# Routing steps of three batches on GpSimd, and pauses between VectorE's steps

## The chip, the cores and the metric

The kernel runs on one core of a Trainium2 chip. The core has TensorE (matmuls), VectorE, ScalarE and GpSimd, each with an instruction queue of its own that is worked off in order, and SyncE, which starts most DMAs. The metric is the device time of one execution in microseconds (us). Executions agree within about 0.2%, so a difference of about 2 us is what can be told from none.

## What is computed

Attention over 4 batches, 8 heads, 576 rows and 64 columns a head, in which a score counts only if it lies within `tau` of its row's maximum; then a mixture of 8 experts, for which each row's expert depends on the row before it; then a normalised feed-forward network with a residual.

```python
thresh = max(scores) - tau                      # per row
attn = softmax(where(scores >= thresh, scores, -1e9)) @ v

logits = x @ w_gate;  local = sigmoid(x @ w_local)
for s in range(S):                              # "sticky" routing, per batch
    e = argmax(logits[s]) if s == 0 or local[s] < 0.5 else prev_e
    prev_e = e
    p = softmax(logits[s])
    out[s] = p[e] * (relu(x[s] @ w1[e]) @ w2[e])

y = x + relu(layernorm(x) * g @ w_ch1) @ w_ch2
```

The routing of a batch turns 576 logit rows into each row's expert, its weight, and its place in a table sorted by expert. It runs on tiles of 128 partitions with 4 to 40 elements each (5 rows a partition, 8 experts), and some of up to 640.

## The kernel before

**Attention.** Work goes in pairs of heads, 16 in all, four to a batch. A pair has 9 *items* of 128 score rows, at positions 0 to 8. One pass of the main loop (`it`) works on several items at once. In a pass VectorE takes the row maximum of one item's scores (`mx`, L403, tile `mc` from `sm`) and masks another item's exponentials (`mask`, L452, `em`); ScalarE takes exponentials (`ex`, L446, `e`) and the upper half of a two-number split (L458, `hl`); GpSimd subtracts to get the lower half (L459, `hl`). TensorE computes the scores for the next maximum (`s_mm`, L399). There is one score tile `sm`, so these matmuls wait until `mx` has read the one before. Then it multiplies with V (`pv`, L474 to L478) for items two and more passes back, and computes transposed scores for the exponential (`t_mm`, L436, L441) into two buffers.

**Around it.** The same passes hold, in an order written out by hand, the preparation of the next pairs' Q, K and V (GpSimd: L306 `nat`, L363 `vl`), and the conversion of the feed-forward weights (`ffn_steps`: three VectorE steps L142, L144, L146 on `cv`, then ScalarE, then GpSimd's L158 `fw`). Conversions stand in the pairs 0 to 5, 7 to 9, 11 and 12. Pairs 6, 10, 13, 14 and 15 start none.

**Routing.** When the last pair of a batch has been stored and gated, `route(b)` runs as a generator: each pass of the loop takes it on to its next `yield`, at the end of the pass. Its matmuls ride in a corner of a score tile, and it goes on two passes later, when that tile's mask has run (`ride`, `alight`). For the first batch it starts in pair 5 at position 6, for the second in pair 9, for the third in pair 13, each time at position 6. The fourth batch's runs after attention, when GpSimd has nothing to do. The steps are named by their output tiles: `mxl`, `fr`, `eq`, `ex8` (with ScalarE's exponential), `eq` again, `idx`, `key`, `hold`, `loc`, the sum `smx`; then `holdr`, `erow`; then `e1`, `oh`; then `rk`, `pe`, `val4`, `pos`, `posi`, `lo`, `hi`; then `ol`, `oc`, `ov`.

Each engine does what its queue holds in the order in which the code was written, so a step that waits holds up everything behind it on its engine.

Of the kernel before, what the change touches and what calls it, by code (L numbers as in the profile page):

```python
# [13 lines left out]
ALU = mybir.AluOpType  # L14
AX = mybir.AxisListType
# [5 lines left out]
def kernel(  # L21
# [15 lines left out]
    nc = tc.nc  # L37
    B, H, S, D = q.shape
# [34 lines left out]
    val4 = const.tile([128, B, 5, 4], F16, name="val4")  # L73
# [156 lines left out]
    if True:  # L230
# [10 lines left out]
        oh = keep.tile([128, 6, 8], F16, name="oh")  # L241
# [318 lines left out]
        def route(b):  # L560


            inner = b < B - 1
# [13 lines left out]
            T = lambda nm, sh, dt=F32: rt_p.tile(sh, dt, name=nm)  # L577
            V = nc.vector
            L = lg[:, :, 0:8]
            mxl = T("mxl", [128, 5])  # L580
            V.tensor_reduce(out=mxl, in_=L, op=ALU.max, axis=AX.X)
            fr = T("fr", [128, 5])
            V.scalar_tensor_tensor(out=fr, in0=lg[:, :, 8], scalar=-1.5 * 2.0 ** -23, in1=first, op0=ALU.is_lt, op1=ALU.max)
            mb = mxl.unsqueeze(2).to_broadcast([128, 5, 8])
            eq = T("eq", [128, 5, 8])
            V.tensor_tensor(out=eq, in0=L, in1=mb, op=ALU.is_equal)
            ex8 = T("ex8", [128, 5, 8])
            V.tensor_tensor(out=ex8, in0=L, in1=mb, op=ALU.subtract)
            nc.scalar.activation(out=ex8, in_=ex8, func=AF.Exp)
# [3 lines left out]
            idx = T("idx", [128, 5])  # L593
            V.tensor_reduce(out=idx, in_=eq, op=ALU.min, axis=AX.X)
            key = T("key", [128, 5], F16)
            V.scalar_tensor_tensor(out=key, in0=idx, scalar=65.0, in1=fr, op0=ALU.add, op1=ALU.mult)
            hold = T("hold", [128, 4])
            V.tensor_scalar(out=hold, in0=key[:, 0:4], scalar1=0.0, scalar2=None, op0=ALU.is_equal)
            loc = T("loc", [128, 4], F16)
            V.tensor_tensor_scan(out=loc, data0=hold, data1=key[:, 0:4], initial=0.0, op0=ALU.mult, op1=ALU.add)  # L600
            sm = T("smx", [128, 5])
# [5 lines left out]

            V.tensor_scalar(out=sm, in0=sm, scalar1=1e-9, scalar2=2.0 ** -15, op0=ALU.add, op1=ALU.mult)
            row = (yield from product(f_row))[0:1, 0:192]
# [10 lines left out]

            V.tensor_tensor(out=ex8, in0=ex8, in1=sm.unsqueeze(2).to_broadcast([128, 5, 8]), op=ALU.mult)
            kb = yield from product(f_kb)
# [10 lines left out]

            V.tensor_tensor(out=ex8, in0=ex8, in1=oh[:, 0:5], op=ALU.mult)
            pe = T("pe", [128, 5])
# [3 lines left out]
            rk = T("rk", [128, 5, 8])  # L639
# [4 lines left out]
            V.tensor_reduce(out=pe, in_=ex8, op=ALU.add, axis=AX.X)  # L644
            V.tensor_tensor(out=rk, in0=rk, in1=oh[:, 0:5], op=ALU.mult)
            V.tensor_copy(out=val4[:, b, :, 1], in_=pe)
            pos = T("pos", [128, 5])
            V.tensor_reduce(out=pos, in_=rk, op=ALU.add, axis=AX.X)
            V.tensor_tensor(out=val4[:, b, :, 3], in0=pe, in1=val4[:, b, :, 1], op=ALU.subtract)
            posi = T("posi", [128, 5], I32)  # L650
            if inner:
                yield
            V.tensor_copy(out=posi, in_=pos)
            if not inner:
# [11 lines left out]
            if inner: yield  # L666
            oc = T("oc", [128, 5, 2 * E], F16)
            V.tensor_tensor(out=oc, in0=colid.unsqueeze(1).to_broadcast([128, 5, 2 * E]), in1=hi.unsqueeze(2).to_broadcast([128, 5, 2 * E]), op=ALU.is_equal)
            ov = T("ov", [128, 5, 4, 2 * E], F16)
            V.tensor_tensor(  # L670
                out=ov, in0=oc.unsqueeze(2).to_broadcast([128, 5, 4, 2 * E]), in1=val4[:, b].unsqueeze(3).to_broadcast([128, 5, 4, 2 * E]), op=ALU.mult)
# [121 lines left out]
    V = nc.vector  # L793
# [588 lines left out]
```

## Time and profile before

| | us |
|---|---|
| runs before, median of 3 (lowest, highest) | 1065.66 (1064.18, 1066.43) |
| the profiled execution | 1066.93 |
| its span, first to last instruction | 1065.0 |
| TensorE busy, matmuls | 999.8 (94%) |
| VectorE busy | 653.1 (61%) |
| ScalarE busy | 506.1 (48%) |
| GpSimd busy | 390.2 (37%) |
| mean granted TensorE clock | 0.971 of full speed |

The profile comes from one execution. In it PE is TensorE, PEld its weight loads, DVE VectorE, ACT ScalarE and POOL GpSimd; L459 is line 459 of the kernel. A busy share over the whole span mixes stages with different limits: attention takes about the first 390 us, and there GpSimd is far busier than its 37%. A bracket behind a row of the timeline gives the idle time of the engine before that instruction, and what ended it. A small instruction's duration contains the time for which it waited for a resource after it was started.

### The profile page before, as it was taken

To read this page: it belongs to the slowest core of one execution; us is meant where nothing else is said; L and a number is where in the kernel's file an instruction comes from. 1 tells how busy PE (TensorE), PEld (TensorE's weight loads), DVE (VectorE), ACT (ScalarE), POOL (GpSimd) and SP (SyncE) were. 2 spreads that over 40 slices of the span, in tenths; PEclk is the share of its full clock that TensorE was granted. 3 is DMA by queue.
4 is the path that set the end of the run, shared out by engine and by line. 5 is a ranking of instruction groups with operands and counts; after the bars stand their busy time and mean duration, and the time that the engine had idled before them with its cause. 6 is when DMAs were issued, how large, how long until landed. Compare 5 with 4: busy or idle time off the path is not lost. (4 is left out here: it accounts for less than half of the span.)

```text
span 1065.0 us, 23705 instructions
## 1 busy us (share of the span) xinstructions
PE 999.8 (94%) x9920; PEld 735.2 (69%) x9920; DVE 653.1 (61%) x1127; ACT 506.1 (48%) x791; POOL 390.2 (37%) x411
## 2 busy tenths in 40 slices
PE   6899998998999978999999979999999999999995
PEld 3678877786888866676667658585768567577572
DVE  7798888988888666697787757274333132231320
ACT  4688886786778655356566545153211011021110
POOL 3689897797788660233222210101000000000000
PEclk8999999999999996899999989999999999999998
DMA  7555634564342735768888765363110210111100
GB/s 177 143 141 148 137 95 125 121 172 129 92 86 57 192 130 171 230 201 276 268 287 306 237 205 167 119 224 117 37 30 31 60 30 31 40 41 41 30 12 22
DMA packets 124533, 137.34 MB, mean 129 GB/s; under 512 B 67450, under 2 KB 88954, under 8 KB 124416
## 3 DMA queue, kind: packets, MB, share of 16 engines
q1 hardware_dynamic: 98336, 116.43, 38.0%
q0 software_dynamic: 4960, 14.17, 3.6%
q10 hardware_dynamic: 21120, 5.13, 2.2%
q8 instruction: 79, 1.29, 0.5%
q14 instruction: 38, 0.31, 0.1%
HBM read 100.17 MB, written 19.94 MB: 113 GB/s over the span
## 5 line engine op out<-in xcount | busy, mean ns | idle before, releaser
L1121 PE MATMUL a<-nT,fw 128*128 128x256 f16 x1728 | 192.5, 274 | 6.3 <-DMA nT<-f 6.3
L1121 PEld LDWEIGHTS <-fw 128*128 128x128 f16 x1728 | 170.1, 98 | 29.3 <-issue 6.8
L459 POOL TENSOR_TENSOR hl<-em,hl 128x576 f16<-128x576 f32 x128 | 169.8, 1327 | 53.6 <-ACT hl L458 52.3
L1134 PE MATMUL y<-fw,hid 128*128 128x512 f16 x864 | 187.9, 379 | 0.0
L1134 PEld LDWEIGHTS <-hid 128*128 128x128 f16 x864 | 84.6, 98 | 100.4
L125 DVE SCALAR_TENSOR_TENSOR w<-stg,w 128x1024 f16<-128x1024 f32 x112 | 134.2, 1221 | 19.6 <-ACT w L124 19.3
L1124 ACT ACTIVATE hid<-a 128x512 f16<-128x512 f32 x72 | 42.7, 593 | 215.9 <-PE a L1121 214.0
L446 ACT ACTIVATE e<-s,t 128x576 f32<-128x576 f32 x144 | 106.2, 737 | 70.7 <-PE s L441 57.5
L1139 POOL DMA_INDIRECT out_dram<-xf x18 | 18.9, 1051 | 311.9 <-DVE xf L1138 311.9
L1012 PE MATMUL a<-xT,w 128*128 128x128 f16 (+1 forms) x1536 | 123.9, 243 | 2.0 <-DVE w L125 0.9
L1012 PEld LDWEIGHTS <-w 128*128 128x128 f16 x1536 | 114.2, 100 | 12.4 <-issue 1.6
L1033 PE MATMUL y<-w,hid 128*128 128x512 f16 x528 | 120.3, 386 | 1.5 <-DVE hid L1017 1.2
L403 DVE TENSOR_REDUCE mc<-sm 128x1 f32<-128x576 f32 x138 | 103.6, 751 | 24.4 <-PE sm L399 22.4
L124 ACT ACTIVATE w<-stg 128x1024 f16<-128x1024 f32 x112 | 114.3, 1051 | 8.8 <-DMA stg<-in_moe_w_dram 5.2
L452 DVE SCALAR_TENSOR_TENSOR em<-s,e 128x576 f32<-128x576 f32 x144 | 107.1, 745 | 9.0 <-POOL hl L459 7.4
L1125 DVE SCALAR_TENSOR_TENSOR hid<-a,hid 128x512 f16<-128x512 f32 x72 | 49.6, 689 | 102.6 <-ACT hid L1124 102.6
L1138 DVE SCALAR_TENSOR_TENSOR xf<-y,xf 128x512 f32<-128x512 f32 x18 | 12.5, 692 | 146.7 <-PE y L1134 146.7
L399 PE MATMUL sm<-qkt 128*128 128x288 f16 (+1 forms) x308 | 75.4, 291 | 24.4 <-DVE mc L403 21.3
L458 ACT ACTIVATE hl<-em 128x576 f16<-128x576 f32 x128 | 87.0, 680 | 18.6 <-DVE em L452 18.0
L1033 PEld LDWEIGHTS <-hid 128*128 128x128 f16 x528 | 51.8, 99 | 62.7 <-issue 3.6
L436 PE MATMUL s<-qkt 128*128 128x288 f16 (+1 forms) x320 | 90.6, 291 | 4.2 <-DVE em L452 3.2
L441 PE MATMUL s<-th,ind 128*128 128x128 bf16 (+5 forms) x960 | 92.6, 207 | 0.0
(288 smaller groups left out, 1805.3 us busy)
## 6 DMA issues: line engine op xcount, KB each, us to landing
stg<-in_moe_w_dram SPq DMA_DIRECT2D x112, 512.0 KB
stg<-in_moe_w_ch_dram SPq DMA_DIRECT2D x32, 512.0 KB
ys_d<-stg SPq DMA_DIRECT2D x6, 769.5 KB
xf<-ys_d SPq DMA_DIRECT2D x9, 513.0 KB
x_d<-xc SPq DMA_DIRECT2D x16, 256.0 KB
ku<-qkt SPq DMA_DIRECT2D x28, 144.0 KB
rawq<-in_q_dram SPq DMA_DIRECT2D x7, 512.0 KB
rawk<-in_k_dram SPq DMA_DIRECT2D x7, 512.0 KB
```

The source lines that it names most:

```text
L124: nc.scalar.activation(out=dst[:, 0, n], in_=t, func=AF.Copy, scale=scale)
L125: nc.vector.scalar_tensor_tensor(out=dst[:, 1, n], in0=t, scalar=scale, in1=dst[:, 0, n], op0=ALU.mult, op1=ALU.subtract)
L403: nc.vector.tensor_reduce(out=mcs[p % 2][:, j:j + 1], in_=mms.pop((p, j))[:, W0:W0 + 576], op=ALU.max, axis=AX.X)
L436: mm(o[:, W0 + 288 * c:W0 + 288 * c + 288], (kt, ku)[k][:, n], y, start=(k == 0), stop=False)
L441: mm(o[:, W0 + i:W0 + i + w], ind[:, t % 4, 0:o.shape[0]], y, start=False, stop=(i == of[-1][0]))
L446: nc.scalar.activation(out=e, in_=mst[p, j][:, W0:W0 + 576], func=AF.Exp, bias=t0, scale=SC)
L452: nc.vector.scalar_tensor_tensor(out=em, in0=ps[:, W0:W0 + 576], scalar=0.0, in1=e, op0=ALU.is_ge, op1=ALU.mult)
L459: nc.gpsimd.tensor_tensor(out=hl[:, 1], in0=em, in1=hl[:, 0], op=ALU.subtract)
L1012: nc.tensor.matmul(ps[:, f, :], t1[:, a, c, fc], x[:, h, i:i + N // 128, c, :], start=(n == 0), stop=(n == 11))
L1033: nc.tensor.matmul(ps, hid[:, x, f, 128 * i:128 * i + 128], t2[:, a, f, :], start=(n == 0), stop=(n == 23))
L1121: nc.tensor.matmul(ps[:, f, :], fw1[:, a, c, fc], x[:, h, :, c, :], start=(n == 0), stop=(n == 11))
L1134: nc.tensor.matmul(ps, hid[:, x, f, ts_], fw2[:, a, f, :], start=(n == 0), stop=(n == 47))
```

## The change

For the first three batches (`inner`) eight steps are issued on GpSimd (`G`) instead of VectorE: the subtraction for `ex8`, `hold`, the scaling of `smx`, the products of `ex8` with `smx` and with `oh`, the product of `rk` with `oh`, the remainder in `val4`, and `ov`. The sum `pos` moves behind the next `yield`. For the first two batches (`b < B - 2`) four more pauses (`gap`) spread VectorE's steps over more passes. The fourth batch's steps stay as they were.

```diff
--- before.py
+++ after.py
@@ -576,26 +576,34 @@
             lg, e1 = lgs[b % 2], e1s[b % 2]
             T = lambda nm, sh, dt=F32: rt_p.tile(sh, dt, name=nm)
             V = nc.vector
+            G = nc.gpsimd if inner else V
+
+            def gap():
+                if b < B - 2:
+                    yield
             L = lg[:, :, 0:8]
             mxl = T("mxl", [128, 5])
             V.tensor_reduce(out=mxl, in_=L, op=ALU.max, axis=AX.X)
             fr = T("fr", [128, 5])
             V.scalar_tensor_tensor(out=fr, in0=lg[:, :, 8], scalar=-1.5 * 2.0 ** -23, in1=first, op0=ALU.is_lt, op1=ALU.max)
             mb = mxl.unsqueeze(2).to_broadcast([128, 5, 8])
+            yield from gap()
             eq = T("eq", [128, 5, 8])
             V.tensor_tensor(out=eq, in0=L, in1=mb, op=ALU.is_equal)
             ex8 = T("ex8", [128, 5, 8])
-            V.tensor_tensor(out=ex8, in0=L, in1=mb, op=ALU.subtract)
+            G.tensor_tensor(out=ex8, in0=L, in1=mb, op=ALU.subtract)
             nc.scalar.activation(out=ex8, in_=ex8, func=AF.Exp)
             yield
             i8 = iota8.unsqueeze(1).to_broadcast([128, 5, 8])
             V.scalar_tensor_tensor(out=eq, in0=eq, scalar=-64.0, in1=i8, op0=ALU.mult, op1=ALU.add)
             idx = T("idx", [128, 5])
             V.tensor_reduce(out=idx, in_=eq, op=ALU.min, axis=AX.X)
+            yield from gap()
             key = T("key", [128, 5], F16)
             V.scalar_tensor_tensor(out=key, in0=idx, scalar=65.0, in1=fr, op0=ALU.add, op1=ALU.mult)
             hold = T("hold", [128, 4])
-            V.tensor_scalar(out=hold, in0=key[:, 0:4], scalar1=0.0, scalar2=None, op0=ALU.is_equal)
+            G.tensor_scalar(out=hold, in0=key[:, 0:4], scalar1=0.0, scalar2=None, op0=ALU.is_equal)
+            yield from gap()
             loc = T("loc", [128, 4], F16)
             V.tensor_tensor_scan(out=loc, data0=hold, data1=key[:, 0:4], initial=0.0, op0=ALU.mult, op1=ALU.add)
             sm = T("smx", [128, 5])
@@ -605,7 +613,7 @@
                 nc.tensor.matmul(t[0:1, 0:128], loc[:, 3:4], ident16)
                 nc.tensor.matmul(t[0:1, 128:192], key[0:64, 4:5], ident16[0:64, 0:64])
 
-            V.tensor_scalar(out=sm, in0=sm, scalar1=1e-9, scalar2=2.0 ** -15, op0=ALU.add, op1=ALU.mult)
+            G.tensor_scalar(out=sm, in0=sm, scalar1=1e-9, scalar2=2.0 ** -15, op0=ALU.add, op1=ALU.mult)
             row = (yield from product(f_row))[0:1, 0:192]
             yield from rest()
             holdr = T("holdr", [1, 192])
@@ -618,7 +626,7 @@
                 nc.tensor.matmul(t[:, 0:1], erow[:, 0:128], one1)
                 nc.tensor.matmul(t[0:64, 4:5], erow[:, 129:193], one1)
 
-            V.tensor_tensor(out=ex8, in0=ex8, in1=sm.unsqueeze(2).to_broadcast([128, 5, 8]), op=ALU.mult)
+            G.tensor_tensor(out=ex8, in0=ex8, in1=sm.unsqueeze(2).to_broadcast([128, 5, 8]), op=ALU.mult)
             kb = yield from product(f_kb)
             yield from rest()
             V.tensor_copy(out=e1[0:64, 4:5], in_=kb[0:64, 4:5])
@@ -631,7 +639,7 @@
                 for i in range(5):
                     nc.tensor.matmul(t[:, 8 * i + 8:48], ones16, oh[:, i:i + 1, :].to_broadcast([128, 5 - i, 8]), start=False, stop=(i == 4))
 
-            V.tensor_tensor(out=ex8, in0=ex8, in1=oh[:, 0:5], op=ALU.mult)
+            G.tensor_tensor(out=ex8, in0=ex8, in1=oh[:, 0:5], op=ALU.mult)
             pe = T("pe", [128, 5])
             R = (yield from product(f_R))[:, 0:48]
             yield from rest()
@@ -642,14 +650,16 @@
                 V.tensor_tensor(out=base_off, in0=R3[:, 5], in1=base_off, op=ALU.add)
                 yield
             V.tensor_reduce(out=pe, in_=ex8, op=ALU.add, axis=AX.X)
-            V.tensor_tensor(out=rk, in0=rk, in1=oh[:, 0:5], op=ALU.mult)
+            G.tensor_tensor(out=rk, in0=rk, in1=oh[:, 0:5], op=ALU.mult)
             V.tensor_copy(out=val4[:, b, :, 1], in_=pe)
             pos = T("pos", [128, 5])
-            V.tensor_reduce(out=pos, in_=rk, op=ALU.add, axis=AX.X)
-            V.tensor_tensor(out=val4[:, b, :, 3], in0=pe, in1=val4[:, b, :, 1], op=ALU.subtract)
+            if not inner:
+                V.tensor_reduce(out=pos, in_=rk, op=ALU.add, axis=AX.X)
+            G.tensor_tensor(out=val4[:, b, :, 3], in0=pe, in1=val4[:, b, :, 1], op=ALU.subtract)
             posi = T("posi", [128, 5], I32)
             if inner:
                 yield
+                V.tensor_reduce(out=pos, in_=rk, op=ALU.add, axis=AX.X)
             V.tensor_copy(out=posi, in_=pos)
             if not inner:
                 V.tensor_tensor(out=base_off, in0=R3[:, 5], in1=base_off, op=ALU.add)
@@ -666,8 +676,9 @@
             if inner: yield
             oc = T("oc", [128, 5, 2 * E], F16)
             V.tensor_tensor(out=oc, in0=colid.unsqueeze(1).to_broadcast([128, 5, 2 * E]), in1=hi.unsqueeze(2).to_broadcast([128, 5, 2 * E]), op=ALU.is_equal)
+            yield from gap()
             ov = T("ov", [128, 5, 4, 2 * E], F16)
-            V.tensor_tensor(
+            G.tensor_tensor(
                 out=ov, in0=oc.unsqueeze(2).to_broadcast([128, 5, 4, 2 * E]), in1=val4[:, b].unsqueeze(3).to_broadcast([128, 5, 4, 2 * E]), op=ALU.mult)
             yield
             def f_A(t):
```

The line numbers in the rows below are those of each kernel; behind the first edits those of the changed one are 5 to 11 higher.

VectorE, first batch, from the pass in which the routing has started. Before:

```order
L588 TENSOR_TENSOR ex8_2978<-lg0_158,mxl_2972 128x40
L403 TENSOR_REDUCE mc_168<-sm_2952 128x1
L452 SCALAR_TENSOR_TENSOR em_2984<-s_2921,e_2945 128x576
L592 SCALAR_TENSOR_TENSOR eq_2976<-eq_2976,iota8_76 128x40
L594 TENSOR_REDUCE idx_3053<-eq_2976 128x5
L596 SCALAR_TENSOR_TENSOR key_3055<-idx_3053,fr_2974 128x5
L598 TENSOR_SCALAR hold_3057<-key_3055 128x4
L600 SCALAR_TENSOR_TENSOR loc_3059<-hold_3057,key_3055 128x4
L602 TENSOR_REDUCE smx_3061<-ex8_2978 128x5
L403 TENSOR_REDUCE mc_168<-sm_2989 128x1
```

And now, from the mask two passes later on:

```order
L452 SCALAR_TENSOR_TENSOR em_3055<-s_2957,e_2977 128x576
L144 SCALAR_TENSOR_TENSOR cv_2701<-stg_2700,cv_2701 128x512
L146 SCALAR_TENSOR_TENSOR cv_2701<-stg_2700,cv_2701 128x512
L598 SCALAR_TENSOR_TENSOR eq_3047<-eq_3047,iota8_76 128x40
L600 TENSOR_REDUCE idx_3129<-eq_3047 128x5
L403 TENSOR_REDUCE mc_168<-sm_3060 128x1
L452 SCALAR_TENSOR_TENSOR em_3134<-s_3032,e_3053 128x576
L603 SCALAR_TENSOR_TENSOR key_3173<-idx_3129,fr_2974 128x5
```

Before, six routing steps stand between one mask and the next maximum (`mc`). Now `eq`'s second step and `idx` stand there, one pass later, where the two conversions of the weights (`cv`) stand too, and `key` stands alone in the pass after.

VectorE, two passes further, with `hold` now computed by GpSimd:

```order
L603 SCALAR_TENSOR_TENSOR key_3173<-idx_3129,fr_2974 128x5
L403 TENSOR_REDUCE mc_168<-sm_3139 128x1
L489 TENSOR_SCALAR rd_3179<-o_2989 128x5
L491 RECIPROCAL rd_3179<-rd_3179 128x5
L452 SCALAR_TENSOR_TENSOR em_3184<-s_3095,e_3132 128x576
L493 TENSOR_TENSOR xc_3178<-o_2989,rd_3179 128x5x64
L608 SCALAR_TENSOR_TENSOR loc_3213<-hold_3175,key_3173 128x4
L610 TENSOR_REDUCE smx_3215<-ex8_3049 128x5
```

`loc` has moved behind the normalisation of the first head's output (`rd`, `xc`).

GpSimd, third batch, around the split of V (`vl`). Before:

```order
L459 TENSOR_TENSOR hl_6746<-em_6744,hl_6746 128x576
L459 TENSOR_TENSOR hl_6780<-em_6778,hl_6780 128x576
L363 TENSOR_TENSOR vl0_157<-vraw_155,vh0_156 128x640
L459 TENSOR_TENSOR hl_6866<-em_6864,hl_6866 128x576
L459 TENSOR_TENSOR hl_6936<-em_6934,hl_6936 128x576
```

And now:

```order
L459 TENSOR_TENSOR hl_6746<-em_6744,hl_6746 128x576
L594 TENSOR_TENSOR ex8_6772<-lg0_158,mxl_6766 128x40
L459 TENSOR_TENSOR hl_6780<-em_6778,hl_6780 128x576
L363 TENSOR_TENSOR vl0_157<-vraw_155,vh0_156 128x640
L605 TENSOR_SCALAR hold_6855<-key_6853 128x4
L459 TENSOR_TENSOR hl_6866<-em_6864,hl_6866 128x576
L616 TENSOR_SCALAR smx_6859<-smx_6859 128x5
```

The third batch has no pauses: VectorE's `loc`, which reads `hold`, stands directly behind `key` there, as before. On GpSimd `hold` stands behind the split of V.

VectorE, first batch's late steps, in the pair with weight conversions that follows pair 6. Before, at its position 2:

```order
L452 SCALAR_TENSOR_TENSOR em_3710<-s_3649,e_3672 128x576
L142 TENSOR_SCALAR cv_3431<-stg_3430 128x512
L668 TENSOR_TENSOR oc_3766<-colid_78,hi_a_111 128x80
L670 TENSOR_TENSOR ov_3768<-oc_3766,val4_79 128x320
L403 TENSOR_REDUCE mc_161<-sm_3715 128x1
L452 SCALAR_TENSOR_TENSOR em_3773<-s_3686,e_3708 128x576
L144 SCALAR_TENSOR_TENSOR cv_3431<-stg_3430,cv_3431 128x512
```

And now, at the same position and the next:

```order
L142 TENSOR_SCALAR cv_3425<-stg_3424 128x512
L652 TENSOR_REDUCE pe_3604<-ex8_3049 128x5
L654 CAST val4_79<-pe_3604 128x5
L403 TENSOR_REDUCE mc_161<-sm_3703 128x1
L452 SCALAR_TENSOR_TENSOR em_3763<-s_3673,e_3693 128x576
L144 SCALAR_TENSOR_TENSOR cv_3425<-stg_3424,cv_3425 128x512
L662 TENSOR_REDUCE pos_3757<-rk_3697 128x5
L663 CAST posi_3759<-pos_3757 128x5
L671 TENSOR_SCALAR lo_a_110<-posi_3759 128x5
L672 TENSOR_SCALAR hi_a_111<-posi_3759 128x5
```

`oc` and `ov` were the routing's last steps there before. Now `pe`, the cast into `val4`, `pos`, `posi`, `lo` and `hi` stand beside the conversions, and the last steps follow later; `pos` reads the `rk` that GpSimd multiplies.

## Rows read from the trace of the kernel before

**Rows 1.** Profile page: engines, busy us, share of span, instructions.
```profile
PE 999.8 (94%) x9920; PEld 735.2 (69%) x9920; DVE 653.1 (61%) x1127; ACT 506.1 (48%) x791; POOL 390.2 (37%) x411
```

**Rows 2.** By stretch: length, busy us PE PEld DVE ACT POOL, clock, DMA, GB/s.
```profile
150.00:205.00 55.00, 49.15 (x696) 40.91 (x696) 48.55 (x98) 38.33 (x65) 39.95 (x41) 1.00 0.43 107
205.00:245.00 40.00, 39.15 (x589) 32.87 (x587) 35.25 (x55) 33.72 (x58) 36.93 (x36) 1.00 0.57 143
245.00:300.00 55.00, 49.54 (x690) 41.30 (x689) 47.76 (x97) 37.29 (x64) 39.12 (x39) 0.97 0.42 106
340.00:388.00 48.00, 43.96 (x648) 37.22 (x647) 36.09 (x85) 31.31 (x52) 32.08 (x35) 0.96 0.52 141
```

**Rows 3.** The same table, two short stretches with TensorE holes.
```profile
256.00:258.00 2.00, 1.35 (x12) 0.98 (x12) 1.97 (x4) 0.71 (x2) 0.00 (x0) 0.52 1.01 175
380.00:382.00 2.00, 0.78 (x16) 0.60 (x12) 2.00 (x3) 0.73 (x2) 0.40 (x1) 1.00 0.00 0
```

**Rows 4.** Timeline, first batch: start us, us, engine, line, operation, tiles.
```profile
157.92 0.94 DVE L596 SCALAR_TENSOR_TENSOR key<-idx,fr 128x5 f16<-128x5 f32 x1
...
158.90 1.21 DVE L598 TENSOR_SCALAR hold<-key 128x4 f32<-128x4 f16 x1
...
160.03 1.36 POOL L363 TENSOR_TENSOR vl<-vraw,vh 128x640 f16<-128x640 f32 x1
160.14 1.27 DVE L600 TENSOR_TENSOR_SCAN loc<-hold,key 128x4 f16<-128x4 f32 x1
```

**Rows 5.** Timeline, VectorE, fourth batch's routing.
```profile
416.94 0.17 DVE L598 TENSOR_SCALAR hold<-key 128x4 f32<-128x4 f16 x1
```

**Rows 6.** Groups by line: operation, tiles, count | busy us, mean ns | idle before.
```profile
L446 ACT ACTIVATE e<-s,t 128x576 f32<-128x576 f32 x144 | 106.2, 737 | 70.7 <-PE s L441 57.5 <-PE s L677 5.6 <-PE s L606 3.5
...
L458 ACT ACTIVATE hl<-em 128x576 f16<-128x576 f32 x128 | 87.0, 680 | 18.6 <-DVE em L452 18.0
...
L158 POOL TENSOR_TENSOR fw<-cv,fw 128x512 f16<-128x512 f32 x22 | 25.6, 1162 | 0.0
...
L414 POOL TENSOR_TENSOR r<-r,pt 128x12 f32<-128x12 f32 x15 | 3.3, 223 | 1.3
...
L867 POOL TENSOR_TENSOR ova<-oca,val 128x1280 f16<-128x1280 f16 x1 | 2.8, 2844 | 10.2 <-DVE oca L865 10.2
```

**Rows 7.** Timeline, third batch: GpSimd, TensorE, VectorE.
```profile
345.62 2.52 POOL L459 TENSOR_TENSOR hl<-em,hl 128x576 f16<-128x576 f32 x2
...
349.38 0.28 PE L399 MATMUL sm<-qkt 128*128 128x288 f16 x1 [1.45 <-DVE mc L403]
...
379.27 1.47 DVE L670 TENSOR_TENSOR ov<-oc,val 128x320 f16<-128x320 f16 x1
```

**Rows 8.** Timeline, VectorE, the pair before routing starts.
```profile
136.21 1.09 DVE L144 SCALAR_TENSOR_TENSOR cv<-stg,cv 128x512 int32<-128x512 int32 x1
137.33 1.65 DVE L146 SCALAR_TENSOR_TENSOR cv<-stg,cv 128x512 int32<-128x512 int32 x1
138.91 0.74 DVE L403 TENSOR_REDUCE mc<-sm 128x1 f32<-128x576 f32 x1
...
147.58 0.74 DVE L403 TENSOR_REDUCE mc<-sm 128x1 f32<-128x576 f32 x1
```

**Rows 9.** Timeline, GpSimd and TensorE, the same pair.
```profile
136.70 1.74 POOL L459 TENSOR_TENSOR hl<-em,hl 128x576 f16<-128x576 f32 x1
138.40 1.80 POOL L363 TENSOR_TENSOR vl<-vraw,vh 128x640 f16<-128x640 f32 x1
...
147.06 1.73 POOL L306 TENSOR_TENSOR nat<-rawq,nat 128x576 f16<-128x576 f32 x1
...
139.71 0.28 PE L399 MATMUL sm<-qkt 128*128 128x288 f16 x1
...
143.90 0.28 PE L399 MATMUL sm<-qkt 128*128 128x288 f16 x1
...
148.91 0.32 PE L399 MATMUL sm<-qkt 128*64 128x288 f16 x2
```

## The prediction, made before the result was known

> **What bounds the kernel now.** I read the engine totals first: TensorE is busy 94% of the span [rows 1], so time is won or lost where TensorE stands still. The table by stretch shows where [rows 2]. From 205 to 245 us, attention without routing, TensorE idles 0.85 us in 40. The stretches that hold the routing of the first three batches idle 5.85 us in 55, 5.46 in 55 and 4.04 in 48. At the rate of 205 to 245 us these would idle 1.2, 1.2 and 1.0, so routing costs 4.7, 4.3 and 3.0 us, 12.0 together. In the second batch the granted clock also fell behind the hole, to 0.52 [rows 3]: TensorE was busy 1.35 us there, of which 0.65 us is lost at half speed; I count 0.7. Nothing that this change does can win more than those 12.7 us.
>
> Then the timelines, for the reason. In the first batch VectorE's `key`, `hold` and `loc`, five elements a row, take 0.94, 1.21 and 1.27 us [rows 4]; in the fourth batch, where GpSimd is idle, `hold` takes 0.17 [rows 5]. `loc` ends at 161.41, when GpSimd's split of V (160.03 + 1.36) has just ended [rows 4]. So a small VectorE step that reads two SBUF tiles, casts, or scales from SBUF to SBUF waits until the GpSimd instruction in progress is over, and then GpSimd's next one runs before VectorE's next one. Five such steps in one item hold back the next `mx`, and TensorE's next scores wait for it.
>
> The Trainium skill, page "SBUF — State Buffer", section "Who interferes with whom", states the same: VectorE and GpSimd share a port pair, whoever starts first has it for the whole instruction, and the other blocks. The trace agrees (1.21 against 0.17 us). The rule speaks against the change as much as for it, since each step given to GpSimd is one more holder; and since it makes every meeting a race, a win by it would rest on who starts first: that is rival 1, 1061 us by the rows below, against the forecast, in which GpSimd does.
>
> **The change, part by part.** Eight steps a batch leave VectorE. On GpSimd seven cost some 0.27 us each (estimate: 0.22 for 12 elements, 1.26 for 576 [rows 6, 7], and these have at most 40) and `ov` 0.7 (2.84 for 1280 columns [rows 6], a quarter of that); 2.6 us a batch, no term by itself. What matters is where they stand in GpSimd's queue, and what waits for them. With the pauses the first two batches take four items more.
>
> I work it out on the pair from 127 to 149 us, which has the same attention work and weight conversions as the pair in which routing starts, and count what routing adds. Positions are those of items in a pair.
>
> *Position 7.* `mxl` and `fr`, two steps of 0.17 (as `hold` [rows 5]), stand ahead of `mx`: TensorE waits 0.35 us.
>
> *Position 8.* `eq` at the end of position 7 meets a GpSimd split and waits for its end: 0 to 1.26 us [rows 7], I take 0.75, a little over half. Then come two conversions and, new here, `eq`'s second step and `idx`. Before, the conversions took 1.09 and 1.65 us with their waits and `mx` began 2.70 us after the first of them [rows 8]; the first ran from 136.70 on, when GpSimd changed instruction [rows 9], so 0.6 of it is work. Now: rest of a split 1.2, conversion 0.6, split of V 1.36 [rows 4], conversion 0.6, the moved `ex8` 0.27, two steps of 0.2: 4.4 us. `mx` is late by 1.7 + 0.75 = 2.5 us, and the scores that began at 139.71 [rows 9] begin at 142.2. Of these 2.5 us 0.35 are counted: 2.15 us.
>
> *Position 2.* `loc` on VectorE now needs `hold` from GpSimd, and ScalarE's `exp` needs `ex8` from GpSimd. `ex8` stands behind the split of V, so `exp` can't start before 141.0 (the new `mx`, 141.4, less the two steps ahead of it); behind it in ScalarE's order wait `e` 0.74 and `hl` 0.68 [rows 6], and for that `hl` GpSimd's next split: 142.6. GpSimd then does that split 1.26, an FFN split 1.16 and another split 1.26 [rows 6, 7] before `hold` 0.27, with VectorE's `key` (0.2) between: 146.7. `loc` and the sum after it take 0.35, `mx` 0.74 and the start of the scores 0.1: 147.9. TensorE would be ready at 143.90 [rows 9] + 2.5 = 146.4. It waits 1.4 us more.
>
> *Position 3 of the pair after next.* The pauses push the last steps out of a pair without weight conversions into one with them. `val`'s cast adds 0.35 to position 2. At position 3 the conversion comes 0.36 us later than it did, so GpSimd's split of Q (from 147.06 [rows 9]) starts first and the conversion waits for all of it, 1.26; then `pos` waits for the moved `rk` step 0.27; `pos`, `posi`, `lo`, `hi` take 0.55. The `mx` that began at 147.58 [rows 8] begins near 149.85; with 0.74 for it the scores begin at 150.6, where TensorE would be ready at 148.91 [rows 9] + 0.35 = 149.2: 1.4 us, with the cast 1.75.
>
> Sum: 0.35 + 2.15 + 1.4 + 1.75 = 5.65 us a batch, against 4.7 in the first and 4.3 + 0.7 in the second: +0.95 and +0.65.
>
> *Third batch.* It has no pauses, so `key`, `loc` and `mx` follow each other, and `loc` waits for a `hold` which stands on GpSimd behind split, `ex8`, split, split of V. The first of two splits that began at 345.62 ends at 346.9 [rows 7]; `ex8` is done at 347.2; ScalarE's `exp` 0.2, `e` 0.74 and `hl` 0.68 give 348.8; split 1.26, split of V 1.36, `hold` 0.27: 351.7. `loc` and the sum 0.3, `mx` 0.74, start 0.1: the scores that began at 349.38 after a wait of 1.45 [rows 7] begin at 352.8. Cost 3.4 us. Behind `loc` in VectorE's order stand `mx` and the mask, so nothing hides it. A hole of 4.9 us is longer than the one behind which the clock fell in the second batch: 0.7 more, bounds 0 and 1.4. Against it, `ov` leaves VectorE where it took 1.47 us and TensorE idled 1.22 [rows 3, 7]: minus 1.2. Net +2.9.
>
> Where I cost at nothing: the moved `smx`, `ex8` products and `val` remainder are wanted an item or more later; if GpSimd is late by more than that, each costs up to 1.3 us, one split. What follows attention starts when TensorE has finished it, so I carry the shift through in full.
>
> Total 0.95 + 0.65 + 2.9 = 4.5 us. The profiled execution took 1066.93 us around a span of 1065.0, 1.3 us above the median 1065.66 of the runs; in those terms 1066.93 + 4.5 = 1071.4, and for the median 1070.2, which I give as 1070 us.
>
> **Rivals.** *1. The spread wins the races (faster).* Place: positions 7 to 2 of the first two batches. If VectorE's single steps start between GpSimd's instructions, each costs 0.17 to 0.2 us, `hold` is done before VectorE has finished its normalisation, and only the 0.35 at position 7 and part of position 3 (0.7) remain: 1.05 instead of 4.7 and 5.0, minus 7.6, and with the third batch's +2.9 the time is 1061. It decides at `loc`: it holds if GpSimd has run `hold` by then. For it: before, five steps met five splits in one item, and now no item has more than two. Against: GpSimd has no gap at 136.70 and 138.40 [rows 9], and the steps land beside two conversions that wait already. If the third batch doesn't pay either, 1058.
>
> *2. Nothing measurable.* First two batches lose what they lose now, because the term at position 3 is hidden by slack in that pair (5.65 - 1.75 = 3.9, -0.8 and -1.1), and the third loses its 2.9: +1.0, 1066.7. For it: the two changes have opposite signs. Against: position 3's scores follow `mx` closely already.
>
> *3. The holes are deeper.* GpSimd falls an item behind and the last pair's products pay too (two splits, 2.6 us in each of the first two batches): +9.7, 1075.4.
>
> That the change doesn't do what it says is excluded: in the new order VectorE has 24 rows less and the steps stand on GpSimd.
>
> **How the numbers follow.** Forecast 0.5, rival 3 0.13, rival 1 0.2, rival 2 0.17. About 0.2%, 2.1 us, is what a measurement can tell from no change. Forecast and rival 3 are slower, except that the lower end of the forecast (a `hold` of the third batch that waits for one split less, -1.3, and a clock that doesn't fall, -0.7) comes to 1068, just outside. Rival 2 lies inside. Chances: slower 0.62, same 0.18, faster 0.2. The forecast's own range is 1068 to 1073. The one that holds 8 in 10 takes in rivals 2 and 3 and the upper part of rival 1: 1062 to 1076.
>
> **What would show it.** In the changed profile: TensorE's scores wait for `mx` in four places in each of the first two batches instead of one long hole, the longest near 2 us; ScalarE's `exp` waits for GpSimd's `ex8`; VectorE's `loc` waits for `hold` on GpSimd, longest in the third batch (about 4 us), with the largest TensorE hole of attention there. The window from 340 us on is some 3 us longer. I am wrong if TensorE's idle time in the first two routing stretches falls below 3 us each, or if `loc` in the third batch starts within 1 us of `key`.

## The result, and the profile after

The changed kernel is slower: 1073.92 us (median of six runs, 1072.53 to 1075.02) against 1064.92 for the kernel before, run beside it. The ratio is 1.0075, its 95% interval 1.0055 to 1.0094, about 8 us (the medians themselves stand 9.0 apart; the six runs before lie between 1063.40 and 1069.24). The forecast was 1070, with a range of 1062 to 1076: the direction and the range held, and the loss was nearly twice the 4.5 us worked out. The profiled execution took 1074.86 us around a span of 1073.0.

The engine line of the page:

```profile
PE 1002.9 (93%) x9920; PEld 737.7 (69%) x9920; DVE 643.8 (60%) x1103; ACT 505.0 (47%) x791; POOL 397.2 (37%) x435
```

Against [rows 1] TensorE is busy 3.1 us longer with the same 9920 matmuls, so the clock was lower in places; the other 4.9 of the 8.0 us between the two spans are idle time. VectorE's busy time fell by 9.3 us, and nothing was gained by that.

The table by stretch, with the columns of [rows 2]:

```profile
150.00:205.00 55.00, 49.01 (x673) 40.31 (x670) 44.83 (x86) 36.49 (x64) 41.09 (x46) 0.95 0.43 105
205.00:245.00 40.00, 39.22 (x583) 32.84 (x582) 34.12 (x55) 33.82 (x59) 35.82 (x36) 0.98 0.57 146
245.00:300.00 55.00, 49.10 (x697) 40.72 (x693) 45.43 (x88) 36.46 (x63) 42.92 (x47) 0.99 0.39 104
340.00:388.00 48.00, 40.96 (x573) 34.36 (x570) 30.46 (x69) 27.77 (x47) 29.85 (x39) 0.92 0.49 135
```

The two stretches of the first two batches idle 5.99 and 5.90 us where they idled 5.85 and 5.46, so the pauses took no idle time away; the granted clock in the first fell to 0.95. The third batch's stretch idles 7.04 instead of 4.04.

A measure that the later comparisons use: the time from pair to pair, read from GpSimd's first small step at the head of each pair of heads (`r` from `mc` and `taus`, line 412, 15 of them). A pair without routing takes 22.1 us. Listed are the three pairs over which a routing stretches, and as "rest" all that follows the head of the third batch's second pair, which is the last pair of attention.

| kernel | ratio to before, 95% | batch 1 | batch 2 | batch 3, first pair | rest |
|---|---|---|---|---|---|
| before | 1 | 26.86 23.45 22.10 | 27.60 23.47 22.06 | 23.37 | 697.5 |
| changed | 1.0075 (1.0055–1.0094) | 25.19 26.54 23.04 | 25.11 25.61 23.05 | 27.89 | 697.4 |
| third batch as before | 1.0029 (1.0013–1.0045) | 25.53 26.54 22.97 | 25.11 25.41 22.97 | 23.30 | 696.2 |
| pauses alone | 1.0018 (1.0002–1.0033) | 28.76 23.99 22.97 | 27.34 23.99 22.98 | 23.36 | 695.3 |
| moves alone | 1.0121 (1.0102–1.0141) | 30.27 24.13 22.08 | 30.39 24.58 22.04 | 28.95 | 698.1 |
| `hold`, `rk`, `ov` back | 1.0002 (0.9989–1.0015) | 25.85 25.57 24.81 | 25.55 25.23 23.96 | 22.56 | 692.0 |
| five steps, third batch | 0.9991 (0.9981–1.0001) | 27.78 23.46 22.09 | 27.81 23.45 22.06 | 22.57 | 694.9 |
| five steps, no pauses | 0.9971 (0.9958–0.9984) | 27.18 24.18 22.10 | 27.09 24.09 22.06 | 22.52 | 694.1 |
| third `hold` back | 1.0034 (1.0021–1.0047) | 25.22 25.57 23.05 | 25.11 25.68 22.93 | 22.56 | 698.2 |
| and `rk` back | 0.9989 (0.9977–1.0001) | 25.21 25.81 23.18 | 25.11 24.37 22.57 | 22.52 | 694.5 |
| and no fourth pause | 0.9976 (0.9961–0.9991) | 25.23 26.01 23.05 | 25.11 24.37 22.71 | 22.52 | 694.1 |

Equal order does not give equal pairs: where batch 1 runs as before (row "five steps, third batch") its first pair took 27.78 instead of 26.86, and the rest came to 695.3 to 697.5 in the three kernels whose third batch is the old one. So differences of a single pair of batches 1 and 2 below 1 us, and of the rest below 2, are not read; the ratios carry the verdicts. From before to changed, the head of the first pair came 0.6 us later, batch 1 cost 2.4, batch 2 0.6, the third batch's first pair 4.5, the rest −0.1: 8.0. The rest falls into two parts at the last mask of attention, the first line from the kernel before, the second from the changed one:

```profile
392.61 0.76 DVE L452 SCALAR_TENSOR_TENSOR em<-s,e 128x576 f32<-128x576 f32 x1 [1.45 <-POOL hl L459]
402.46 0.76 DVE L452 SCALAR_TENSOR_TENSOR em<-s,e 128x576 f32<-128x576 f32 x1 [1.45 <-POOL hl L459]
```

The last pair, up to the end of that mask, grew from 25.9 to 27.6 us; what follows it fell from 671.6 to 669.8. Behind that mask all the engines have the same order in both kernels, and in the eleven traces that part takes 667.1 to 671.6 us, so the 1.9 us gained there are chance, not the change.

The timeline of the third batch, as in [rows 7]:

```profile
350.39 0.26 POOL L594 TENSOR_TENSOR ex<-lg,mxl 128x40 f32<-128x40 f32 x1
...
350.69 0.24 ACT L595 ACTIVATE ex<-ex 128x40 f32<-128x40 f32 x1 [2.49 <-POOL ex L594]
...
350.76 0.17 DVE L603 SCALAR_TENSOR_TENSOR key<-idx,fr 128x5 f16<-128x5 f32 x1
...
352.20 1.28 POOL L459 TENSOR_TENSOR hl<-em,hl 128x576 f16<-128x576 f32 x1 [1.55 <-ACT hl L458]
...
353.44 1.35 POOL L363 TENSOR_TENSOR vl<-vraw,vh 128x640 f16<-128x640 f32 x1
...
354.76 0.22 POOL L605 TENSOR_SCALAR hold<-key 128x4 f32<-128x4 f16 x1
...
355.01 0.17 DVE L608 TENSOR_TENSOR_SCAN loc<-hold,key 128x4 f16<-128x4 f32 x1 [4.08 <-POOL hold L605]
...
356.00 0.28 PE L399 MATMUL sm<-qkt 128*128 128x288 f16 x1 [4.53 <-DVE mc L403]
```

`ex8` waits on GpSimd behind a split, `exp` waits 2.49 us for it, and the next split (352.20) waits for the `hl` that stands behind `exp`. `hold` is issued behind that split and the split of V, and starts 4.00 us after `key`. `loc` waits 4.08 us and takes 0.17; the scores start after 4.53 us in which TensorE had nothing.

The first batch, where before had one hole of 0.86 us and this one:

```profile
162.22 0.28 PE L399 MATMUL sm<-qkt 128*128 128x288 f16 x1 [3.11 <-DVE mc L403]
```

And now:

```profile
156.64 0.28 PE L399 MATMUL sm<-qkt 128*128 128x288 f16 x1 [0.58 <-DVE mc L403]
...
163.16 0.24 ACT L595 ACTIVATE ex<-ex 128x40 f32<-128x40 f32 x1 [3.31 <-POOL ex L594]
...
164.13 0.28 PE L399 MATMUL sm<-qkt 128*128 128x288 f16 x1 [1.27 <-DVE mc L403]
...
168.55 0.17 DVE L608 TENSOR_TENSOR_SCAN loc<-hold,key 128x4 f16<-128x4 f32 x1 [0.57 <-POOL hold L605]
...
169.54 0.28 PE L399 MATMUL sm<-qkt 128*128 128x288 f16 x1 [0.78 <-DVE mc L403]
```

Three holes of 0.58, 1.27 and 0.78 us. `loc` waits only 0.57 us for `hold`: the pause ahead of it has given GpSimd nearly the time it needed.

The pair after next of the same batch, at position 3:

```profile
195.18 1.84 POOL L306 TENSOR_TENSOR nat<-rawq,nat 128x576 f16<-128x576 f32 x1
...
196.97 0.26 POOL L653 TENSOR_TENSOR rk<-rk,oh 128x40 f32<-128x40 f32 x1
...
197.26 0.20 DVE L662 TENSOR_REDUCE pos<-rk 128x5 f32<-128x40 f32 x1 [1.39 <-POOL rk L653]
...
197.50 1.15 DVE L663 CAST posi<-pos 128x5 int32<-128x5 f32 x1
...
199.63 0.46 PE L399 MATMUL sm<-qkt 128*64 128x288 f16 x2 [2.23 <-DVE mc L403]
```

The split of Q holds up the moved `rk` step, `pos` waits 1.39 us for that step, `posi` then meets the next split for 1.15, and the scores wait 2.23 us. Behind this hole the clock fell, in batch 2 behind an equal one too:

```profile
198.00:200.00 2.00, 0.37 (x4) 0.36 (x5) 1.97 (x5) 0.09 (x1) 0.62 (x1) 0.84 0.02 4
200.00:202.00 2.00, 2.00 (x18) 1.17 (x14) 1.64 (x3) 0.68 (x1) 0.96 (x1) 0.50 0.00 0
202.00:204.00 2.00, 2.00 (x19) 1.49 (x17) 1.18 (x4) 0.00 (x0) 0.31 (x1) 0.50 0.04 8
204.00:206.00 2.00, 2.00 (x12) 1.55 (x11) 1.01 (x4) 1.71 (x3) 0.32 (x1) 0.50 0.17 23
298.00:300.00 2.00, 2.00 (x19) 1.56 (x18) 1.75 (x6) 0.00 (x0) 1.09 (x1) 0.59 0.00 0
300.00:302.00 2.00, 2.00 (x13) 1.54 (x13) 1.01 (x4) 1.86 (x4) 0.47 (x1) 0.56 0.27 31
```

At 200 to 206 us TensorE is busy all the time at 0.50, the lower of its two levels (1.2 GHz); that loses 3.0 us. In batch 2 two slices at 0.59 and 0.56 lose 1.7.

The third batch's late steps:

```profile
382.29 0.26 POOL L653 TENSOR_TENSOR rk<-rk,oh 128x40 f32<-128x40 f32 x1
...
382.58 0.20 DVE L662 TENSOR_REDUCE pos<-rk 128x5 f32<-128x40 f32 x1 [0.81 <-POOL rk L653]
...
383.08 1.19 DVE L669 TENSOR_TENSOR base_off<-base_off,reg 128x2 f32<-128x2 f32 x1
...
386.15 0.30 PE L436 MATMUL s<-qkt 128*128 128x288 f16 x1 [1.97 <-DVE em L452]
```

`pos` waits for `rk` here as well, and `base_off` behind it meets another split. `rd` and the mask for TensorE stand behind these on VectorE: a hole of 1.97 us. In the kernel before, the scores behind the same mask (the one that follows `rd`) waited 0.38 us:

```profile
376.44 0.30 PE L436 MATMUL s<-qkt 128*128 128x288 f16 x1 [0.38 <-DVE em L452]
```

The hole that `ov` used to end [rows 3], 1.22 us at 381.46 and two masks further on, is gone: behind the 1.97 the changed kernel has no hole of 0.3 us up to 396.97.

### The profile page after: what moved, and what is told of

It is laid out like the page before. It is cut to its first block, busy times and chain, and to the rows that moved or that the text cites. A ratio compares the mean times of both kernels' runs of the same rounds, so it can differ in the third digit from the quotient of the medians.

```text
span 1073.0 us, 23701 instructions
## 1 busy us (share of the span) xinstructions
PE 1002.9 (93%) x9920; PEld 737.7 (69%) x9920; DVE 643.8 (60%) x1103; ACT 505.0 (47%) x791; POOL 397.2 (37%) x435
## 5 line engine op out<-in xcount | busy, mean ns | idle before, releaser
L459 POOL TENSOR_TENSOR hl<-em,hl 128x576 f16<-128x576 f32 x128 | 167.6, 1310 | 56.5 <-ACT hl L458 55.3
```

The source lines that it names most:

```text
L459: nc.gpsimd.tensor_tensor(out=hl[:, 1], in0=em, in1=hl[:, 0], op=ALU.subtract)
```

## Experiments

Theory W: the loss is waiting for single results of GpSimd, which come in the order of its queue, behind splits. Rivals: L, that GpSimd is simply loaded more with every step; P, that the pauses, which push late steps beside conversions, are the loss.

**Third batch as before.**

```diff
-            G = nc.gpsimd if inner else V
+            G = nc.gpsimd if b < B - 2 else V
```

(and `pos` ahead of the `yield` for that batch.)

> The third batch runs as before (all eight steps on VectorE, the sum pos ahead of the yield); batches 1 and 2 as changed. Theory W (waits): the loss comes from VectorE and ScalarE waiting for single results of GpSimd, above all loc for hold in the third batch, whose first pair is 4.5 us longer in the changed kernel's trace. Then this kernel is 4.5 us faster than the changed one, about 1069.5 us (+0.4% on before). Rival L (load): every step given to GpSimd lengthens its queue by the same amount, 8.0 us over 24 steps; then a third of the loss goes, 1071.2. Rival P (pauses): the four pauses shift the late steps into pairs with conversions and that is the loss; then nothing goes, 1073.9.

1.0029, some 3.1 us above before, so about 4.9 us of the 8.0 went with the third batch. Its first pair is back at 23.30. This suits W (1069.5 by its number); L's 2.7 us lies just within the uncertainty of the two ratios. P is out as the whole cause.

**Pauses alone.**

```diff
-            G = nc.gpsimd if inner else V
+            G = V
```

> The four pauses in batches 1 and 2 alone; all steps stay on VectorE, pos ahead of the yield as before. W: the one hole of 3.1 us in each batch's first pair is spread, 1.7 to 2.5 us won there as in the changed kernel; in the next pair the late steps beside the conversions cost some 1.5 us, but pos waits for nobody on GpSimd; net about -0.5 us a batch, 1064. L: no step moved, nothing lost: also 1064 to 1065. P: the loss of batches 1 and 2 in the changed kernel's trace, 2.4 + 0.6, shows here in full or more: 1068.

1.0018: 0.2 to 3.5 us slower. W's forecast of a small gain failed, P's 3 us is inside, L's zero just outside. The trace says why there is no gain:

```profile
158.83 1.32 DVE L594 TENSOR_TENSOR ex<-lg,mxl 128x40 f32<-128x40 f32 x1
...
161.40 1.78 DVE L144 SCALAR_TENSOR_TENSOR cv<-stg,cv 128x512 int32<-128x512 int32 x1
...
164.79 1.15 DVE L598 SCALAR_TENSOR_TENSOR eq<-eq,iota 128x40 f32<-128x40 f32 x1
...
166.88 0.40 PE L399 MATMUL sm<-qkt 128*128 128x288 f16 x1 [2.45 <-DVE mc L403]
```

`ex8`, still on VectorE, meets a split (1.32 us) and puts the first conversion off to 161.40, 1.9 us later than in the changed kernel (0.6 of it because the whole pair runs later), so `eq` and `idx` behind the conversions come late and the scores wait 2.45 us. In these runs the pauses shorten the first pair only where `ex8` is on GpSimd.

**Moves alone.** At four places:

```diff
-            yield from gap()
```

> The eight steps on GpSimd in three batches, pos behind the yield, but no pause. W: each batch's first pair now has loc directly behind key with hold behind GpSimd's splits, so each pays about what the third paid: 3 times 4 to 4.5 us, 1077 to 1078, slower than the changed kernel. L: as the changed kernel, 1073.9. P: only the third batch's 4.5 us remain, 1069.5.

1.0121, 12.9 us: three times 4.3. In batch 1:

```profile
163.64 0.24 POOL L600 TENSOR_SCALAR hold<-key 128x4 f32<-128x4 f16 x1
...
163.92 0.17 DVE L602 TENSOR_TENSOR_SCAN loc<-hold,key 128x4 f16<-128x4 f32 x1 [4.57 <-POOL hold L600]
...
164.91 0.40 PE L399 MATMUL sm<-qkt 128*128 128x288 f16 x1 [5.43 <-DVE mc L403]
```

The same wait as in the third batch, 4.57 us, ends in a hole of 5.43. W holds; L and P are out, since the same steps on GpSimd cost 5 us more without the pauses.

**`hold`, `rk` and `ov` back on VectorE**, pauses and the other five steps as changed.

```diff
-            G.tensor_scalar(out=hold, ...
+            V.tensor_scalar(out=hold, ...
-            G.tensor_tensor(out=rk, ...
+            V.tensor_tensor(out=rk, ...
-            G.tensor_tensor(out=ov, ...
+            V.tensor_tensor(out=ov, ...
```

> As changed, but hold, the product of rk and ov stay on VectorE (pos ahead of the yield as before); the other five steps stay on GpSimd, pauses as changed. W: the two waits that end in TensorE holes are gone (loc for hold, pos for rk); what is left is exp waiting for ex8, about +1 in the third batch, against the spread's gain in batches 1 and 2, about -1.5 each: 1062 to 1065, no slower than before. L: 15 of 24 moved steps remain, 5 us of the loss: 1070. P: batches 1 and 2 lose as in the changed kernel, 3 us: 1068.

1.0002: the whole loss is gone with 15 of 24 steps still on GpSimd. L is out. `exp` was expected to cost 1 us in the third batch; instead its first pair is 22.56, as in the five other kernels with `hold` on VectorE and `ex8` on GpSimd there (22.52 to 22.57), against 23.30 to 23.37 in the three with the old third batch. The gain of 1.5 us a batch that W expected in batches 1 and 2 is not in the trace: their pairs take 76.2 and 74.7 us, against 72.4 and 73.1 before. The rest (692.0) makes up for it, and 4.6 of its 5.5 us lie behind attention, where the order is the same. So for these two batches this run does not refute P.

**The five steps in the third batch only**, `hold`, `rk` and `ov` on VectorE as in the run above; batches 1 and 2 as before.

```diff
-            G = nc.gpsimd if inner else V
+            G = nc.gpsimd if b == B - 2 else V
...
-            yield from gap()
```

> Batches 1 and 2 as before the change; in the third batch five steps go to GpSimd (ex8, smx, both ex8 products, the remainder), while hold, the product of rk and ov stay on VectorE. Theory W (only a step whose result VectorE, ScalarE or TensorE wants at once costs): the third batch's first pair comes to 22.6 us as where hold stayed on VectorE (23.4 before), and the last pair and the fourth batch lose a hole or two (0.9 to 5 us in that run): 1 to 6 us faster than before, forecast 3. Rival L (load on GpSimd): five steps more on GpSimd, 1 to 2 us slower.

0.9991, between 2.0 us faster and 0.1 slower: less than the forecast 3, and not told from no change. The first pair came to 22.57 as expected. L's 1 to 2 us slower is excluded.

**The five steps in all three batches, no pauses**; `hold`, `rk` and `ov` on VectorE again.

```diff
-            G.tensor_scalar(out=hold, ...
+            V.tensor_scalar(out=hold, ...
...
-            yield from gap()
```

> The same five steps on GpSimd in all three batches, no pauses, hold, rk and ov on VectorE. W: the first pair of batches 1 and 2 wins as the third batch's does, 0.8 us each, and the clock does not fall in the pairs with conversions, because no late step stands there: 4.5 us faster than before. Rival E: without the pauses exp, which waits for ex8 on GpSimd, delays the scores of the next item as in the run with all moves and no pauses (first pairs 30.3 us); with hold back on VectorE that leaves some 28 us, 1 us above before, in two batches: 1 us faster than before at most.

0.9971: 3.1 us faster than before (1.7 to 4.5), a version that beats both kernels. E's 1 us is outside. Against the run with `hold`, `rk` and `ov` back, which differs by the four pauses alone, it is 3.3 us (1.3 to 5.3, from the intervals of both ratios): with these five moves the pauses cost time, so P is right for that part. Batch 1:

```profile
160.47 0.26 POOL L590 TENSOR_TENSOR ex<-lg,mxl 128x40 f32<-128x40 f32 x1
...
160.57 0.18 DVE L600 TENSOR_SCALAR hold<-key 128x4 f32<-128x4 f16 x1
...
160.78 0.17 DVE L602 TENSOR_TENSOR_SCAN loc<-hold,key 128x4 f16<-128x4 f32 x1
...
161.94 0.28 PE L399 MATMUL sm<-qkt 128*128 128x288 f16 x1 [1.27 <-DVE mc L403]
...
166.59 0.28 PE L399 MATMUL sm<-qkt 128*128 128x288 f16 x1 [1.08 <-DVE mc L403]
```

`ex8` on GpSimd still makes `exp` late, but `hold` and `loc` take 0.18 and 0.17 on VectorE, and the two longest holes are 1.27 and 1.08 us instead of one of 3.11. The late steps stay out of the pair with conversions, and the clock doesn't fall at 200 us; it does fall behind the hole of 1.08 (0.61 and 0.54 in the two slices from 168 us), and the first pairs are not clearly shorter than before (27.18 and 27.09), where W expected 0.8 us each. So where the 3.1 us lie is only partly shown: 0.8 in the third batch's first pair and 1.6 in the last pair of attention; the profiled execution (1065.49 us against a median of 1062.57) was one of the slower ones, and up to the end of attention it is no shorter than that of before.

**The changed kernel with the third batch's `hold` on VectorE.**

```diff
-            G.tensor_scalar(out=hold, ...
+            (G if b < B - 2 else V).tensor_scalar(out=hold, ...
```

> The changed kernel with one edit: in the third batch hold is computed by VectorE again. W: the wait of loc for hold, 4.08 us in the changed kernel's trace, is the third batch's loss; the first pair goes from 27.9 back to 23 to 24 us and the clock does not fall behind it: 4 to 5 us faster than the changed kernel, about 0.35% slower than before. Rival X: the delay is ex8, behind which exp and the next heads' e and hl wait; then loc only changes what it waits for, and at most 1.5 us come back.

1.0034 instead of 1.0075: 4.4 us (1.9 to 6.9) by one instruction of 4 columns. The first pair is 22.56. X, which allowed 1.5 us at most, is out: `ex8` is still on GpSimd. (The profiled execution, 1072.58 us, was the slowest of the twelve, so its rest of 698.2 is not typical.) The first line shows what is left of the hole; the others are the late steps:

```profile
354.53 0.28 PE L399 MATMUL sm<-qkt 128*128 128x288 f16 x1 [0.76 <-DVE mc L403]
...
379.30 0.25 POOL L653 TENSOR_TENSOR rk<-rk,oh 128x40 f32<-128x40 f32 x1
...
379.59 0.20 DVE L662 TENSOR_REDUCE pos<-rk 128x5 f32<-128x40 f32 x1 [0.80 <-POOL rk L653]
...
379.82 2.09 DVE L663 CAST posi<-pos 128x5 int32<-128x5 f32 x1
...
383.25 0.42 PE L436 MATMUL s<-qkt 128*128 128x288 f16 x1 [2.35 <-DVE em L452]
```

**And the product of `rk` back on VectorE**, `pos` ahead of the `yield`.

```diff
-            G.tensor_tensor(out=rk, ...
+            V.tensor_tensor(out=rk, ...
```

> As the run with the third batch's hold on VectorE, and besides the product of rk with oh on VectorE in all three batches, pos ahead of the yield. Theory W: pos no longer waits for GpSimd. In the third batch the hole of 2.35 us ahead of the scores at 383 us shrinks to 0.5 us or less and the clock does not fall behind it (5 us at half speed in that run); in the pair after next of batches 1 and 2 the hole of 2.23 us becomes 1.6, as where all three of hold, rk and ov were on VectorE. Together 3 to 5 us faster than that run: within 0.1% of before. Rival Q: those holes come from the conversions and the split of Q that stand there, not from pos; then they stay at 2.2 to 2.4 and the time at 0.3% above before.

0.9989 against 1.0034: 4.8 us more (2.9 to 6.7), and no slower than before.

```profile
199.18 0.32 PE L399 MATMUL sm<-qkt 128*64 128x288 f16 x2 [1.57 <-DVE mc L403]
...
295.37 0.32 PE L399 MATMUL sm<-qkt 128*64 128x288 f16 x2 [1.58 <-DVE mc L403]
...
373.43 0.18 DVE L656 TENSOR_REDUCE pos<-rk 128x5 f32<-128x40 f32 x1
...
376.65 0.30 PE L436 MATMUL s<-qkt 128*128 128x288 f16 x1 [0.37 <-DVE em L452]
```

The third batch's hole fell from 2.35 to 0.37 us, those at position 3 from 2.23 to 1.57 and 1.58. Q is out for the third batch. The run takes back two things at once, the product and the place of `pos` behind the `yield`; what each gives alone was not run. For position 3 both are right: 0.65 us is `pos`'s wait, 1.6 is the conversions and splits beside the late steps, which the pauses moved there.

**And without the fourth pause**, the one ahead of `ov`.

```diff
-            yield from gap()
             ov = T("ov", [128, 5, 4, 2 * E], F16)
```

> As the run before it in this list, without the fourth pause (the one ahead of ov): ov and the accumulator's product come one item earlier, back into the pair in which they stood before the change. W: the third pair of batches 1 and 2 falls from 23.0 to 22.1 us and the second pair takes up the product's 0.5 us: 0.5 us a batch won, 1 us in all. Rival: ov on GpSimd beside the conversions delays the product wherever it stands, and the sum of the two pairs does not change: 0.

0.9976 against 0.9989, a difference within the uncertainty. The trace is on the rival's side: second and third pair of batch 1 come to 48.99 before and 49.06 now, and the accumulator's product, the routing's last matmuls (`ov` with `ol`), still stands in the third pair, which starts at 204.7 us (in the kernel before it ran at 201.63, in the second pair):

```profile
209.00 0.50 PE L685 MATMUL s<-ov,ol 128*128 128x32 f16 x10
```

What the other 20 steps on GpSimd and three pauses give against before is 2.6 us (1.0 to 4.2).

## Why the prediction was right, and where it was not

*What bounds the kernel.* Right: the whole change shows as holes of TensorE (4.9 us) and a lower clock behind them (3.1). The price of the clock in the kernel before was read too low, though. Behind the hole of batch 2 the prediction counted the slice from 256 us (0.7); the next one lost as much again:

```profile
258.00:260.00 2.00, 2.00 (x34) 1.86 (x33) 2.00 (x3) 0.50 (x1) 1.95 (x2) 0.63 0.92 288
```

The 0.96 of the third batch's stretch [rows 2] was not counted at all.

*Third batch, `loc` for `hold`.* Right in mechanism: a wait of about 4 us was named, 4.08 came; scores waiting 4.85 (1.45 + 3.4), 4.53 came. The clock behind it was under-sized: two slices at 0.60 and 0.55 lose 1.7 us, where 0.7 was counted and 1.4 was the bound. In sum 4.1 us was forecast, and the pair grew by 4.5. The run that takes `hold` alone back gives 4.4.

*Third batch, `ov` leaving VectorE, −1.2.* This step failed. The hole that `ov` ended did go, but the prediction did not ask what the other moved steps put into the same pair: `pos` waits for `rk` behind a split, a step that it charged to the first two batches only, and the hole of 0.38 us there became 1.97, with a fall of the clock behind it (0.78, 0.50 and 0.87 in the slices from 386 us). The last pair grew by 1.7 us instead of shrinking by 1.2. With `rk` and the place of `pos` taken back the hole fell from 2.35 to 0.37 us, the fall of the clock that stood behind it in the run with only `hold` back (0.64, 0.50, 0.50 and 0.66 in the four slices from 382 us) is gone, and the rest went from 698.2 to 694.5. Nor did the hole need `ov` to leave: in the two five-step kernels `ov` is on VectorE, the longest hole between 352 and 389 us is 0.52, and the rest is 694.1 to 694.9.

*Positions 7, 8 and 2.* The waits stand where they were put, but are smaller: 0.58, 1.27 and 0.78 us, together 2.63, against 0.35, 2.15 and 1.4, together 3.9. Over-sized was position 8: the conversions did take 1.7 us each beside GpSimd's splits, but from the first of them (159.54) to the next `mx` (163.33) 3.8 us passed, where 4.4 were forecast. At position 2 the prediction's own times give 147.9 − 146.4 = 1.5, not 1.4. The first pairs became shorter, by 1.7 and 2.5 us, twice what these terms gave against before's 4.7 and 5.0.

*Position 3 of the pair after next.* Under-sized: 1.75 forecast, 0.35 + 2.23 us of holes came. The split of Q was taken at 1.26 us, though its row has 1.73 [rows 9] and it took 1.84 here. And the clock's fall behind the hole, 3.0 and 1.7 us, was counted for the third batch but not here. That made batch 1 cost 2.4 instead of 0.95: over its three pairs TensorE idles 6.3 us against 6.2 before, so the loss there is the clock's. Batch 2 cost 0.64 against 0.65, which is luck: before's own fall of the clock, which went away, was counted at half its price, and the new fall was not counted.

The sum: 1.4 us too little in batch 1, 0.4 in the third batch's first pair, 2.9 in the last pair, 0.6 at the start of the kernel, where the change does nothing, and 1.9 too much behind attention, where it does nothing either: 3.4 us, the difference between 4.5 and 8.0 but for 0.1.

*Rivals.* Rival 1 (races won) came true in the first pairs, which are 1.7 and 2.5 us shorter, and was paid back in the next. Rival 2 (nothing) is out. The time lies just above the forecast's own 1068 to 1073 and nearer to rival 3's 1075.4, but not for rival 3's reason: it put 2.6 us more into each of the first two batches, and what came beyond the forecast is the clock in batch 1 and the third batch's last pair. So the range held in part because errors of both signs met. The Trainium skill, page "GPSIMD Engine Reference", section "Engine selection", advises VectorE for element-wise work on a tile, because GpSimd is about twice as slow with two inputs. The trace agrees in direction only: the product of `rk` takes 0.26 us on GpSimd and 0.19 on VectorE where it is undisturbed. Its speed, 0.07 us apart, is not what cost 4.8 us; where it stands in the queue, and `pos` behind it, is.

## What to carry to other kernels

Ask of each step that is to move to a busy in-order engine who waits for its result and how soon; a step with a consumer in the same item costs all that is queued ahead of it there, here 4 us for a step of 0.22, while `ex8`'s products, the scaling and the remainder, wanted an item later, moved at no cost that these runs show. Undo single moves before undoing the idea: taking back two of the eight, one of them in the third batch alone, removed the loss, and five moves without pauses beat the kernel before. Pauses are no gain by themselves: alone they cost 1.9 us, beside five moves 3.3; beside the eight moves, where they give GpSimd time for `hold`, they save 4.9 (12.9 without them, 8.0 with them). Where a hole of TensorE is priced, price the clock behind it at every hole, not only at the longest.

## What was not expected of the hardware

The clock's fall does not follow from the length of the hole alone. In the run with `hold` and `rk` back, TensorE idled 1.57 us at 199 us and was then granted 0.50 for the three 2-us slices from 200 to 206; after an equal hole of 1.58 us at 295 in the same run the slices up to 310 stayed at 1.00. Behind the 4.53 us hole of the third batch only two slices fell, to 0.60 and 0.55.

GpSimd instructions that only write seem to hold VectorE too; this is read from equal ends, no run tests it. In the changed kernel `lo` started at 384.19 us together with GpSimd's two fills of `xg`; it took 1.01 us and ended as they did (384.19 + 0.99), and `hi` and `rd` behind it (0.95 and 0.88) ended with it. With `rk` back on VectorE, where the fills came later, `lo` took 0.17. In the run with only the third `hold` back, `posi` (2.09 us) and the step behind it (1.01) ended with the fills too (380.90 + 0.99).
